# Attention and mixer kernel on one core: four small transfers moved to ScalarE's queue, and the last two batches and the late weight decoding in another order

## The chip, the cores and the metric

The kernel runs on one core of a Trainium2 chip. The metric is device time in microseconds (us). TensorE is written PE, VectorE DVE, ScalarE ACT, GpSimd POOL and SyncE SP. PEld is TensorE's loading of stationary operands, which overlaps PE.

## The reference

Eight batches of eight heads of causal attention with a decay, over 576 positions of 64 channels, and behind it a token mixer and a channel mixer:

```python
scores = q @ k.T / sqrt(64) + cum[:, None] - cum[None, :]   # cum = cumsum(log(clip(f)))
attn   = softmax(where(causal, scores, -1e9))
x      = concat_heads(attn @ v)                             # 8 x 576 x 512
h      = relu(x.T @ w_tok1) @ w_tok2                        # 576 -> 256 -> 576, over positions
u      = x + h.T
out    = u + relu(u @ w_ch1) @ w_ch2                        # 512 -> 1536 -> 512
```

Everything is float32. The four weights reach the kernel as 64-bit floats, in pairs of 32-bit words, and are decoded on the chip.

## The kernel before, in words

**Two-part products.** Most matrix products split a float32 operand into a high part and a rest (the tiles ending in h and l, or `p`, `hid`, `ring`, which hold both). ACT copies the high part (L351), and DVE (L360, or L363 with a ReLU) or POOL (L357) subtracts it from the operand. Three matmuls then stand for one.

**One head.** Q and K of a pair of heads arrive as `raw`, are split into `hl` (L546 and L556 or L548 and L556), and are gathered by SP transfers (L600) into the operands `k1` and `k2`. Rows of the decay come from `cc`, the running sum of log f, by small transfers (L594). PE makes the scores (L627), DVE masks them and takes row minima (L634), ACT takes exponentials (L641), DVE makes reciprocals (L659, L662) and POOL scales the rows (L669). PE transposes them (L683), ACT and DVE split them (L351, L360), and PE multiplies by V (L753 to L765). The products go into `xt` (L803 to L813). The first two heads are different (`FQ=2`): Q and K go into `xt`'s second tile as plain float32 (L604), and their two decay rows each are four transfers of one row (L589).

**The mixer of one batch.** In two halves: transposes (L984), first token product (`tok1`, L1017 to L1020) with its ReLU (L363), second (`tok2`, L1041 to L1043), the sum with x (L1055), then on the first 256 hidden channels `ch1` (L1086 to L1088) with its ReLU, and `ch2` (L1114 to L1116). The sums go to DRAM (`ud`, `pd`).

**The last part.** The other 1280 hidden channels are done after all attention, in nine chunks of 512 columns. A chunk has ten steps. The step's "up" is twelve matmuls with `w1r` (L900 to L902), then a ReLU split into `hid` (ACT L351, DVE L363), and its "down" is twelve with `w2r` (L921 to L923).

**Late decoding.** `w1r` and `w2r`, ten of each, are decoded into space that attention has used, so it can't begin before the last heads have let go of their buffers. Each of the 20 pieces is loaded as `d_raw` (L429), taken by ACT (L441), worked on by DVE in five instructions of 512 columns (L445, L449, L453, L457, L461), copied by ACT (L351) and completed by DVE (L360): six DVE instructions a piece. The first of a kernel's weights (`w_tok`) go the same way early, in smaller pieces, with POOL doing two of the steps.

**What sets the order.** The kernel's Python code lists operations with a priority, a duration, the tiles that they need, and what they wait for. `Plan.run` (L188) then plays them on five engines: a free engine takes the ready operation with the lowest priority number. The order that results is what is built, and each engine works through its list in that order. The priorities come from tables of numbers: `STEP` by head, `EARLY` and `LATE` added for the first and the last batch, `MIX` with `MIXE` and `MIXL` for the mixer, and `DEC3` as the spacing of the late pieces (L837). Durations in the plan only shape the order.

**SP's transfers.** SP issues transfers in order. Each transfer belongs to one of eight counters (`DMAHW0` to `DMAHW7`), and is issued only when the earlier transfer on the same counter has landed.

Of the kernel before, what the change touches and what calls it, by code (L numbers as in the profile page):

```python
# [20 lines left out]
    n_ring=12, n_part=4, n_xt=2, n_d_raw=3, n_d_g=2, n_hid=3, DEC3=10.1, SPREAD=9.86, SPREADA=5.54,  # L21
# [4 lines left out]
    fpe=3.69, lo0=-44.75, fev=-192.41, u=-110.56, dec=70.59, dec2=33.11, dec3=34.58, cd=-12.6, vload=-16.33,  # L26
# [113 lines left out]
class Op:  # L140
    __slots__ = ("eng", "dur", "head", "tail", "lat", "fn", "prio", "bufs", "need", "outs", "ready", "start", "idx")


class Plan:
# [43 lines left out]
    def run(self, slots):  # L188
# [9 lines left out]
        n = 0  # L198
# [8 lines left out]
        tail = dma_at = 0.0  # L207
# [30 lines left out]
        while left:  # L238
            moved = False
            for e, lst in ready.items():  # L240
# [23 lines left out]
                engine_at[e] = end  # L264
                heapq.heappush(events, (end, heap_id, None))
# [44 lines left out]
def build(nc, env, dims):  # L310
# [60 lines left out]

    def decay():
# [50 lines left out]
    def decode(prio, loads, w, hi, lo, tok, late=None):  # L423
# [15 lines left out]
        def s1():  # L439
            low, high, g, e = tl()  # L440
            nc.scalar.activation(asf(g), asf(high), AF.Copy, scale=2.0**-112)  # L441
# [23 lines left out]
        p.op("DVE", d_dve(w, True) * (1.2 if late else 1.8), prio, s3, rd=[gb], wr=[(gb, 1)], bufs=[gb])  # L465
        p.op("DVE", d_dve(w) * (1.1 if late else 1.3), prio, s4, rd=rd, wr=[(gb, 1)], bufs=[rb, gb])
        p.op("DVE" if late else "POOL", d_dve(w) if late else d_ptt(w), prio, s5, rd=[(gb, 1)], wr=[gb], bufs=[gb])
        p.op("DVE", d_dve(w), prio, s6, rd=rd, wr=[gb], bufs=[rb, gb])
        p.op("ACT", d_act(w, False), prio, lambda: hi_act(hi(), asf(tl()[2])), rd=[gb, *([late] if late else [])], wr=[(tok, "h")], bufs=[gb])
        p.op(  # L470
# [366 lines left out]
    for i, fn in enumerate(third):  # L837
        fn(HB + 2 + PRM["DEC3"] * i + (OFF["dec3"] if i < 2 * PAIRS0 else 0.0))
# [464 lines left out]
```

## Time and profile before

| | |
|---|---|
| three runs | 1123.4, 1130.65, 1132.02 us; median 1130.65 |
| profiled execution | 1124.72 us; its span is 1122.6 us, so 2.1 us lie around it |
| busy | PE 1080.8, DVE 633.9, ACT 557.3, POOL 536.5 us |
| attention with its mixers | to about 625 us of the span |
| nine chunks of the last part | from there to the end |

The granted clock (PEclk) is TensorE's clock as a share of full speed. In this trace it is 1.00 or 0.50, with values between where a window holds both. A row of the timeline gives the start, the duration, the engine and line, what was done, and in brackets how long the engine had been idle and what ended that. Timelines merge neighbouring instructions of one line, with their count behind an x. A row of the windows view gives for a stretch its length, the busy time of each engine with instruction counts, the granted clock, the DMA engines' busy share, and GB/s.

### The profile page before, as it was taken

To read this page: it belongs to the slowest core of one execution; us is meant where nothing else is said; L and a number is where in the kernel's file an instruction comes from. 1 tells how busy PE (TensorE), PEld (TensorE's weight loads), DVE (VectorE), ACT (ScalarE), POOL (GpSimd) and SP (SyncE) were. 2 spreads that over 40 slices of the span, in tenths; PEclk is the share of its full clock that TensorE was granted. 3 is DMA by queue.
4 is the path that set the end of the run, shared out by engine and by line. 5 is a ranking of instruction groups with operands and counts; after the bars stand their busy time and mean duration, and the time that the engine had idled before them with its cause. 6 is when DMAs were issued, how large, how long until landed. Compare 5 with 4: busy or idle time off the path is not lost.

```text
span 1122.6 us, 18731 instructions
## 1 busy us (share of the span) xinstructions
PE 1080.8 (96%) x6442; PEld 943.4 (84%) x6442; DVE 633.9 (56%) x1618; ACT 557.3 (50%) x1441; POOL 536.5 (48%) x615
## 2 busy tenths in 40 slices
PE   7898989999999999999998899999999999999998
PEld 5567878999999999998998788888888888888886
DVE  5778989787878877887799971121212121111111
ACT  3776868788888878887884531111111111111110
POOL 4577897869778678786843103230303121111010
PEclk8898999999999999999998999999999999999999
DMA  8687877777787787786724514230303030302011
GB/s 212 148 206 147 206 192 206 210 187 193 194 203 203 178 210 190 193 220 151 183 105 139 184 61 142 69 114 1 113 1 112 1 112 1 113 11 65 21 55 38
DMA packets 70831, 148.43 MB, mean 132 GB/s; under 512 B 10008, under 2 KB 27416, under 8 KB 69712
## 3 DMA queue, kind: packets, MB, share of 16 engines
q1 hardware_dynamic: 70736, 147.23, 48.7%
q8 instruction: 51, 0.84, 0.3%
q14 instruction: 44, 0.36, 0.1%
HBM read 63.46 MB, written 28.31 MB: 82 GB/s over the span
## 4 chain that ended last, share of the span: by engine, by line
PE 76%; DMA 8%; DVE 6%; POOL 3%; SPq 3%; ACT 2%; issue 2%; DVEq 0%; ACTq 0%; POOLq 0%
PE bank L901 7%; PE bank L900 7%; PE bank L902 7%; PE pair L922 7%; PE pair L921 7%; PE pair L923 7%; DMA k<-hl 6%; PE bank L683 6%; PE bank L627 5%; PE pair L627 2%; PE pair L765 2%; PE pair L763 2%; POOL pr L669 2%; SPq L600 1%; PE bank L1017 1%
## 5 line engine op out<-in xcount | busy, mean ns | idle before, releaser
L363 DVE SCALAR_TENSOR_TENSOR hid<-bank,hid 128x512 fp32r<-128x512 f32 x90 | 62.2, 691 | 340.5 <-ACT hid L351 340.4
L357 POOL TENSOR_TENSOR ring<-xt,ring 128x512 fp32r<-128x512 f32 (+1 forms) x68 | 91.9, 1365 | 316.7 <-ACT ring L351 315.9
L351 ACT ACTIVATE hid<-bank 128x512 fp32r<-128x512 f32 x90 | 53.9, 599 | 342.7 <-PE bank L902 342.7
L669 POOL TENSOR_SCALAR pr<-pr,rec 128x576 f32<-128x576 f32 (+4 forms) x320 | 171.8, 556 | 42.6 <-DVE rec L662 33.2
L351 ACT ACTIVATE p<-bank 128x384 fp32r<-128x384 f32 (+2 forms) x300 | 128.4, 475 | 48.0 <-PE bank L683 46.3
L683 PE MATMUL bank<-ident,pr 128*128 128x128 f32 (+1 forms) x960 | 140.3, 280 | 2.2 <-POOL pr L669 1.4
L900 PE MATMUL bank<-ring,w1r 128*128 128x512 f32 x360 | 140.1, 389 | 0.0
L901 PE MATMUL bank<-ring,w1r 128*128 128x512 f32 x360 | 140.1, 389 | 0.0
L902 PE MATMUL bank<-ring,w1r 128*128 128x512 f32 x360 | 140.1, 389 | 0.0
L921 PE MATMUL pair<-hid,w2r 128*128 128x512 f32 x360 | 140.1, 389 | 0.0
L922 PE MATMUL pair<-hid,w2r 128*128 128x512 f32 x360 | 140.0, 389 | 0.0
L923 PE MATMUL pair<-hid,w2r 128*128 128x512 f32 x360 | 140.0, 389 | 0.0
L641 ACT ACTIVATE pr<-bank,nmin 128x320 f32<-128x320 f32 (+3 forms) x256 | 118.1, 469 | 24.0 <-DVE nmin L634 22.1
L683 PEld LDWEIGHTS bank<-ident,pr 128*128 128x128 f32 (+1 forms) x960 | 109.5, 133 | 14.0 <-issue 3.4
L360 DVE TENSOR_TENSOR p<-bank,p 128x384 fp32r<-128x384 f32 (+1 forms) x180 | 106.0, 593 | 26.7 <-ACT p L351 25.6
L634 DVE CUSTOM_DVE_ANT_0 bank<-bank,mask 64x64 f32<-64x64 f32 (+3 forms) x256 | 106.7, 433 | 21.5 <-PE bank L627 19.2
L627 PE MATMUL bank<-k 128*128 128x320 f32 (+1 forms) x496 | 91.2, 305 | 10.9 <-DMA k<-hl 5.9
L627 PEld LDWEIGHTS bank<-k 128*128 128x128 f32 x496 | 76.9, 182 | 25.0 <-DMA k<-hl 5.3
L876 POOL TENSOR_TENSOR part<-part,xt 128x512 f32<-128x512 f32 x36 | 46.5, 1300 | 77.3 <-DMA part<-pd 71.7
L921 PEld LDWEIGHTS pair<-hid,w2r 128*128 128x128 f32 x360 | 67.6, 188 | 14.1
L923 PEld LDWEIGHTS pair<-hid,w2r 128*128 128x128 f32 x360 | 67.6, 188 | 14.1
L901 PEld LDWEIGHTS bank<-ring,w1r 128*128 128x128 f32 x360 | 67.6, 188 | 13.9
(125 smaller groups left out, 2482.7 us busy)
## 6 DMA issues: line engine op xcount, KB each, us to landing
k<-hl SPq DMA_DIRECT2D x186, 288.0 KB
raw<-in_qk SPq DMA_DIRECT2D x31, 576.0 KB
vr<-in_v SPq DMA_DIRECT2D x32, 320.0 KB
ud<-xt SPq DMA_DIRECT2D x8, 1152.0 KB
pd<-part SPq DMA_DIRECT2D x32, 288.0 KB
out_t<-part SPq DMA_DIRECT2D x36, 256.0 KB
d_raw<-in_w_ch SPq DMA_DIRECT2D x12, 512.0 KB
d_raw<-in_w_ch SPq DMA_DIRECT2D x40, 128.0 KB
```

Of the source, the lines that this page charges most:

```text
L351: nc.scalar.activation(out, in_, func, scale=scale)
L627: nc.tensor.matmul(ps[:m, of : of + w], k[:, 0, i0 : i0 + m], k[:, 1, j0 : j0 + w], start=(x == 0), stop=(fq or x == 1))
L634: nc.vector.tensor_tensor_reduce(x, x, E["mask"][:m, a : a + w], -1.0 / D**0.5, 3e38, op0=ALU.add, op1=ALU.min, accum_out=E["nmin"][sm][:m ...
L641: nc.scalar.activation(at(pr)[:m, poff[t] : poff[t] + w], at(buf)[:m, of : of + w], AF.Exp, bias=E["nmin"][sm][:m, t : t + 1], scale=-1.0, ...
L669: nc.gpsimd.tensor_scalar(x, x, r, 0.0, op0=ALU.mult, op1=ALU.add)
L683: nc.tensor.transpose(out, at(pr)[:, poff[i] + start[j] : poff[i] + end[j]], E["ident"])
L900: nc.tensor.matmul(q, wh[:, c, :], h_, start=(c == 0), stop=False)
L901: nc.tensor.matmul(q, wl[:, c, :], h_, start=False, stop=False)
L902: nc.tensor.matmul(q, wh[:, c, :], l_, start=False, stop=(c == NC - 1))
L921: nc.tensor.matmul(q, wh, h_, start=(i == i0), stop=False)
L922: nc.tensor.matmul(q, wl, h_, start=False, stop=False)
L923: nc.tensor.matmul(q, wh, l_, start=False, stop=(i == NF - 1))
```

## The change

Four edits.

1. The four transfers of the float32 heads' decay rows leave SP's queue. ACT issues them, right ahead of its first instruction of the first decoded piece (`t1`, position 0). The plan still counts them on SP.
2. The tables. `EARLY`, `LATE`, `MIXE` and `MIXL` become `HEAD` and `MIXB`, with one row for each batch. The row of batch 0 holds `EARLY`'s numbers, those of batches 1 to 5 hold zeros as before, and those of batches 6 and 7 are new. `DEC3` goes from 10.1 to 26.65 and `OFF["dec3"]` from 34.58 to 78.27, which spreads the late pieces over larger priority numbers.
3. From batch 6 on (`PORT = 6`) the plan doesn't start an operation of POOL, or a DVE operation marked `port` (the decoding's DVE steps, and the subtraction in L556 where DVE does it), before the end that the plan has set for the last such operation. This is a rule of the plan alone. No wait is added in the program that runs.
4. In the late decoding the plan's factors of 1.2 and 1.1 on three DVE durations become 1.0.

```diff
-    n_ring=12, n_part=4, n_xt=2, n_d_raw=3, n_d_g=2, n_hid=3, DEC3=10.1, SPREAD=9.86, SPREADA=5.54,
+    n_ring=12, n_part=4, n_xt=2, n_d_raw=3, n_d_g=2, n_hid=3, DEC3=26.65, SPREAD=9.86, SPREADA=5.54,
...
-    fpe=3.69, lo0=-44.75, fev=-192.41, u=-110.56, dec=70.59, dec2=33.11, dec3=34.58, cd=-12.6, vload=-16.33,
+    fpe=3.69, lo0=-44.75, fev=-192.41, u=-110.56, dec=70.59, dec2=33.11, dec3=78.27, cd=-12.6, vload=-16.33,
...
-EARLY = dict(
...
-LATE = dict(
...
+HEAD = dict(
+    cd=(
+        (42.22, -3.16, 15.37, -9.18, 55.25, -12.47, -73.68, 11.62),
+        (0.0, 0.0, 0.0, 0.0, 0.0, 0.0, 0.0, 0.0),
...
+        (-18.17, 6.86, 10.93, -1.41, -16.23, 1.17, 0.15, -28.59),
+        (-0.06, -1.59, -4.28, -6.54, -12.25, 0.0, 32.34, 3.06),
+    ),
...
+PORT = 6
...
+        o.port = (port or eng == "POOL") and self.batch >= PORT
...
-                    if o.ready > t or (best is not None and (o.prio, o.idx) >= (best.prio, best.idx)):
+                    if o.ready > t or (o.port and port_at > t) or (best is not None and (o.prio, o.idx) >= (best.prio, best.idx)):
...
+                if o.port:
+                    port_at = end
...
         def s1():
             low, high, g, e = tl()
+
+            for k, n, x in fqr if tok == ("t1", first_tok) else ():
+                nc.scalar.dma_start(at(k)[D + x : D + x + 1, x, :], asf(at(cc)[n : n + 1, 2, :]))
             nc.scalar.activation(asf(g), asf(high), AF.Copy, scale=2.0**-112)
...
+        m2, m1 = (1.2, 1.1) if p.batch < PORT else (1.0, 1.0)
...
-        p.op("DVE", d_dve(w, True) * (1.2 if late else 1.8), prio, s2, wr=[gb], bufs=[gb])
+        p.op("DVE", d_dve(w, True) * (m2 if late else 1.8), prio, s2, wr=[gb], bufs=[gb], port=True)
...
-        o = {k: OFF[k] + x[h] + (EARLY[k][h] if b == 0 else 0.0) + (LATE[k][h] if b == B - 1 else 0.0) for k, x in STEP.items()}
+        p.batch = b
+        o = {k: OFF[k] + x[h] + HEAD[k][b % 8][h] for k, x in STEP.items()}
...
             if fq:
+
+                fqr.append((k2, n, x))
                 dma(
-                    n + o["cd"], lambda k2=k2, n=n, x=x: nc.sync.dma_start(at(k2)[D + x : D + x + 1, x, :], asf(at(cc)[n : n + 1, 2, :])),
+                    n + o["cd"], lambda: None,
                     2304, dur=650, rd=["c", "rows"], wr=[(k2, "d", x)], bufs=[k2, cc],
                 )
...
     for i, fn in enumerate(third):
+        p.batch = B if i >= 3 else 0
         fn(HB + 2 + PRM["DEC3"] * i + (OFF["dec3"] if i < 2 * PAIRS0 else 0.0))
```

The lists of the two programs, engine by engine, are the same up to batch 6, but for the four transfers. The rows below have the line number of their own program: L589 is L670 in the changed one, L568 is L800, L594 is L828, L600 is L834, L441 is L671, L546 is L777, L351 is L575, L360 is L584, L363 is L587, L1055 is L1290, and L445, L449, L453, L457 and L461 are L675, L679, L683, L687 and L691.

**SP at the start**, before. `xt_130` holds the float32 heads, `cc_178` the decay sums; `hl` to `k` are the gathers of the third and fourth heads.

```order
L594 DMA k_164<-cc_178 2x1x576 [waits DMAHW5_49]
L589 DMA xt_130<-cc_178 1x16x36 [waits DMAHW6_49]
L589 DMA xt_130<-cc_178 1x16x36 [waits DMAHW7_49]
L568 DMA raw_158<-in_qk 128x1152 [waits DMAHW0_49,DVE_49]
L600 DMA k_162<-hl_161 64x1152 [waits DMAHW1_49]
L600 DMA k_164<-hl_161 64x2x576 [waits DMAHW2_49]
L589 DMA xt_130<-cc_178 1x16x36 [waits DMAHW3_49]
L589 DMA xt_130<-cc_178 1x16x36 [waits DMAHW4_49]
L600 DMA k_162<-hl_161 64x2x576 [waits DMAHW5_49]
L600 DMA k_163<-hl_161 64x2x576 [waits DMAHW6_49]
```

In the changed program the four L589 rows are gone from SP, and ACT has them between the split of the first `hl` and the first decoding:

```order
L777 ACTIVATE hl_161<-raw_158 128x2x576 [waits DMAHW1_49]
L670 DMA xt_130<-cc_178 1x16x36 [waits DMAHW0_49,DVE_49,Pool_49]
L670 DMA xt_130<-cc_178 1x16x36 [waits DMAHW2_49,Pool_49]
L670 DMA xt_130<-cc_178 1x16x36 [waits DMAHW4_49]
L670 DMA xt_130<-cc_178 1x16x36 [waits DMAHW6_49]
L671 ACTIVATE d_g_146<-d_raw_143 128x256 [waits DMAHW5_49]
L671 ACTIVATE d_g_147<-d_raw_144 128x256
```

The two rows of the second float32 head (the last two on each list) move ahead of two gathers. On ACT they stand behind counters 4 and 6, whose earlier transfers are the first and the third of the four loads of `d_raw`.

**DVE at the end of `tok1` of batch 7**, before. The ReLU of `tok1` is `ring_137<-bank_65,ring_136`; `tok2` on PE waits for it.

```order
L360 TENSOR_TENSOR ring_141<-bank_68,ring_141 64x256
L1055 TENSOR_TENSOR xt_130<-bank_67,xt_130 128x288
L453 SCALAR_TENSOR_TENSOR d_g_146<-d_raw_144,d_g_146 128x512
L445 TENSOR_SCALAR d_g_147<-d_g_147 128x512
L457 TENSOR_TENSOR d_g_146<-d_g_146 128x512
L449 TENSOR_SCALAR d_g_147<-d_g_147 128x512
L461 SCALAR_TENSOR_TENSOR d_g_146<-d_raw_144,d_g_146 128x512
L453 SCALAR_TENSOR_TENSOR d_g_147<-d_raw_143,d_g_147 128x512
L363 SCALAR_TENSOR_TENSOR ring_137<-bank_65,ring_136 128x512
```

And in the changed program:

```order
L584 TENSOR_TENSOR ring_141<-bank_68,ring_141 64x256
L1290 TENSOR_TENSOR xt_130<-bank_66,xt_130 128x288
L1290 TENSOR_TENSOR xt_130<-bank_67,xt_130 128x288
L584 TENSOR_TENSOR w1r_6911<-d_g_146,w1r_6911 128x512
L675 TENSOR_SCALAR d_g_147<-d_g_147 128x512
L587 SCALAR_TENSOR_TENSOR ring_137<-bank_65,ring_136 128x512
```

Six instructions of the late decoding stood between the last sum and the ReLU, and now two.

**DVE between `ch1` and `ch2` of batch 7**, before. The first two L363 rows are the ReLU results that `ch2` on PE waits for.

```order
L449 TENSOR_SCALAR d_g_146<-d_g_146 128x512
L453 SCALAR_TENSOR_TENSOR d_g_146<-d_raw_145,d_g_146 128x512
L445 TENSOR_SCALAR d_g_147<-d_g_147 128x512
L457 TENSOR_TENSOR d_g_146<-d_g_146 128x512
L449 TENSOR_SCALAR d_g_147<-d_g_147 128x512
L461 SCALAR_TENSOR_TENSOR d_g_146<-d_raw_145,d_g_146 128x512
L453 SCALAR_TENSOR_TENSOR d_g_147<-d_raw_144,d_g_147 128x512
L457 TENSOR_TENSOR d_g_147<-d_g_147 128x512
L360 TENSOR_TENSOR w2r_7145<-d_g_146,w2r_7145 128x512
L363 SCALAR_TENSOR_TENSOR ring_137<-bank_67,ring_136 128x288
L363 SCALAR_TENSOR_TENSOR ring_142<-bank_66,ring_141 128x288
```

And in the changed program:

```order
L1290 TENSOR_TENSOR xt_130<-bank_65,xt_130 128x288
L691 SCALAR_TENSOR_TENSOR d_g_146<-d_raw_143,d_g_146 128x512
L687 TENSOR_TENSOR d_g_147<-d_g_147 128x512
L587 SCALAR_TENSOR_TENSOR ring_137<-bank_67,ring_136 128x288
L587 SCALAR_TENSOR_TENSOR ring_142<-bank_66,ring_141 128x288
L587 SCALAR_TENSOR_TENSOR ring_137<-bank_65,ring_136 128x288
```

Nine decoding instructions stood between the last sum and the ReLU, and now two. The work put off comes later: of the 120 DVE instructions of the late decoding, 64 stood ahead of the first `hid` row (L363, the ReLU split of the first up step), and now 48. Between the first `hid` row and the end of the last `w1r` piece there were 59 DVE rows in all (both ends counted), and now 77. PE's list around this place keeps its shape: 28 matmuls of `tok1`, 24 of `tok2`, 48 of `ch1`, 30 of `ch2`, then up, up, down, up, down and so on.

More of the change, by code (lines that the diff above doesn't have):

```diff
@@ L107 @@
+HEAD = dict(
+    cd=(
[8 rows of a table added]
+    ),
+    kh=(
[8 rows of a table added]
+    ),
+    kl=(
[8 rows of a table added]
+    ),
+    s4=(
[8 rows of a table added]
+    ),
+    s3=(
[8 rows of a table added]
+    ),
+    s2=(
[8 rows of a table added]
+    ),
+    mn=(
[8 rows of a table added]
+    ),
+    ex=(
[8 rows of a table added]
+    ),
+    rec=(
[8 rows of a table added]
+    ),
+    nrm=(
[8 rows of a table added]
+    ),
+    t3=(
[8 rows of a table added]
+    ),
+    t2=(
[8 rows of a table added]
+    ),
+    t1=(
[8 rows of a table added]
+    ),
+    t0=(
[8 rows of a table added]
+    ),
+    hl=(
[8 rows of a table added]
+    ),
+    av=(
[8 rows of a table added]
+    ),
+    fold=(
[8 rows of a table added]
+    ),
+    load=(
[8 rows of a table added]
+    ),
+    vload=(
[8 rows of a table added]
+    ),
+    qh=(
[8 rows of a table added]
+    ),
+    ql=(
[8 rows of a table added]
+    ),
+    vh=(
[8 rows of a table added]
+    ),
+    vl=(
[8 rows of a table added]
+    ),
+    lo0=(
[8 rows of a table added]
+    ),
 )
@@ L140 @@
 class Op:
-    __slots__ = ("eng", "dur", "head", "tail", "lat", "fn", "prio", "bufs", "need", "outs", "ready", "start", "idx")
+    __slots__ = ("eng", "dur", "head", "tail", "lat", "fn", "prio", "bufs", "need", "outs", "ready", "start", "idx", "port")
 class Plan:
@@ L461, in s6 @@
             nc.vector.scalar_tensor_tensor(g, high, 0x80000000, g, op0=ALU.bitwise_and, op1=ALU.bitwise_or)
+        m2, m1 = (1.2, 1.1) if p.batch < PORT else (1.0, 1.0)
         p.op("ACT", d_act(w, False), prio, s1, rd=rd, wr=[gb], bufs=[rb, gb])
[L464 to L468 removed]
+        p.op("DVE", d_dve(w, True) * (m2 if late else 1.8), prio, s2, wr=[gb], bufs=[gb], port=True)
+        p.op("DVE", d_dve(w, True) * (m2 if late else 1.8), prio, s3, rd=[gb], wr=[(gb, 1)], bufs=[gb], port=True)
+        p.op("DVE", d_dve(w) * (m1 if late else 1.3), prio, s4, port=True, rd=rd, wr=[(gb, 1)], bufs=[rb, gb])
+        p.op("DVE" if late else "POOL", d_dve(w) if late else d_ptt(w), prio, s5, port=True, rd=[(gb, 1)], wr=[gb], bufs=[gb])
+        p.op("DVE", d_dve(w), prio, s6, port=True, rd=rd, wr=[gb], bufs=[rb, gb])
         p.op("ACT", d_act(w, False), prio, lambda: hi_act(hi(), asf(tl()[2])), rd=[gb, *([late] if late else [])], wr=[(tok, "h")], bufs=[gb])
@@ L572, in build @@
                 el, d_lo(el, 2 * S), n + o["ql"], lambda hl=hl, raw=raw, el=el: lo_on(el, at(hl)[:, 1::2, :], at(raw), at(hl)[:, 0::2, :]),
-                rd=[raw, (hl, 0)], wr=[(hl, 1)], bufs=[hl, raw],
+                rd=[raw, (hl, 0)], wr=[(hl, 1)], bufs=[hl, raw], port=True,
             )
@@ L1135, in mixer @@
     for i, (c, f) in enumerate(us):
-        f(n + 1 + PRM["LAG"] + o["fpe"] + MIX[part][i] + (MIXE[part][i] if b == 0 else 0.0) + (MIXL[part][i] if b == B - 1 else 0.0) + (PRM["SPREAD"] if part else PRM["SPREADA"]) * done / total)
+        f(n + 1 + PRM["LAG"] + o["fpe"] + MIX[part][i] + MIXB[b % 8][part][i] + (PRM["SPREAD"] if part else PRM["SPREADA"]) * done / total)
         done += c
```

98 lines of the change are left out of this document (39 added, 59 removed), and 188 rows, old and new, of tables (av, cd, ex, fold).

## The prediction

> **What bounds the kernel now.** I read the page first, then the windows, then the timelines of single engines where PE stops.
>
> ```profile
> span 1122.6 us, 18731 instructions
> ...
> PEclk8898999999999999999998999999999999999999
> ```
>
> ```profile
> 0.00:28.00 28.00, 22.27 (x175) 16.12 (x175) 15.71 (x46) 11.01 (x26) 13.37 (x26) 0.84 0.86 212
> 252.00:280.00 28.00, 28.00 (x219) 26.92 (x218) 21.88 (x67) 24.00 (x67) 25.51 (x32) 1.00 0.73 188
> 588.00:616.00 28.00, 24.58 (x171) 24.18 (x170) 25.77 (x40) 12.87 (x23) 8.72 (x6) 0.88 0.42 146
> 616.00:644.00 28.00, 23.99 (x114) 20.57 (x113) 27.66 (x48) 14.53 (x28) 4.47 (x4) 0.94 0.54 171
> 644.00:672.00 28.00, 28.00 (x125) 23.21 (x124) 22.37 (x40) 9.89 (x16) 0.00 (x0) 1.00 0.23 75
> ```
>
> In the middle and in the last part PE is busy all the time at full clock: the end moves with PE's lost time and with nothing else. PE loses time at the start and in the handover to the last part, both by pauses and by a halved clock. In the handover DVE is almost full, so PE's pauses there are DVE's. Each us that PE gains at one of these places reaches the end, if nothing behind it makes PE wait again.
>
> **The start: the decay rows.**
>
> ```profile
> 14.91 2.71 SPq L589 DMA_DIRECT2D xt<-cc  x2
> 17.67 1.34 SPq L600 DMA_DIRECT2D k<-hl  x2
> ```
>
> ```profile
> 15.73 6.11 DMA xt<-cc
> ```
>
> ```profile
> 15.86 2.23 PE L627 MATMUL bank<-xt 66*128 66x448 f32 x8
> 21.97 3.95 PE L627 MATMUL bank<-xt 66*128 66x320 f32 x8 [3.88 <-DMA xt<-cc]
> 25.85 2.24 PE L627 MATMUL bank<-k 128*128 128x320 f32 x8
> ```
>
> The second head's rows are issued at 14.91 and 15.73, and the last lands 6.11 us later; PE has nothing from 18.09 (15.86 and 2.23) to 21.97. The change issues them on ACT. How early, and what do they push?
>
> ```profile
> 7.11 1.15 ACT L546 ACTIVATE hl<-raw 128x1152 fp32r<-128x1152 f32 x1
> 10.28 0.81 ACT L441 ACTIVATE d_g<-d_raw 128x256 f32<-128x256 f32 x2 [2.03 <-DMA d_raw<-in_w_tok]
> 18.76 0.30 ACT L641 ACTIVATE pr<-bank,nmin 64x64 f32<-64x64 f32 x1
> ```
>
> ```profile
> 15.77 0.59 DVE L445 TENSOR_SCALAR d_g<-d_g 128x256 uint32<-128x256 uint32 x1 [0.81 <-ACT d_g L441]
> 16.29 0.75 DVE L634 CUSTOM_DVE_ANT_0 pair<-pair,mask 128x576 f32<-128x576 f32 x1
> ```
>
> ACT is free at 8.26 and idles for 2.03 us until `d_raw` has landed. The first two transfers fit there. The other two wait on counters whose earlier transfers are loads of `d_raw`, so they go out at about 10 to 10.7. ACT's price for one isn't in the trace; the nearest rows are SP's, 0.67 for a gather (1.34 for two). ACT starts decoding at about 11.3, 1.0 us later (bounds 0 and 1.4). The first head's rows aren't missed, since PE works through its warm-up matmuls until then. Those of the second, even at 6.11 us from an issue at 11.3, land at 17.4, ahead of 18.09.
>
> What is late next? The decode chain is pushed by 1.0 us, and L445 at 15.77 stands ahead of the first head's minima (16.29) on DVE. The exponentials follow by the same 1.0, and PE's next eight matmuls write the bank that the exponential at 18.76 frees, at 19.06. So PE resumes near 20.2 and not at 21.97: **1.75 us**. The third head's gathers are no new wait. The first SP row behind the moved ones, 17.67, goes out nearly 4 us earlier, and PE wants its data only after eight matmuls.
>
> The clock is the other half.
>
> ```profile
> 20.00:24.00 4.00, 2.03 (x5) 1.67 (x6) 0.58 (x3) 0.68 (x3) 3.04 (x6) 0.50 1.04 239
> ...
> 32.00:36.00 4.00, 4.00 (x24) 3.21 (x25) 3.62 (x13) 3.18 (x10) 1.82 (x3) 0.90 0.02 6
> ```
>
> The mean of 0.90 puts the return to full speed at 32.8. From 21.97 that is 10.8 us at half speed, a loss of 5.4 us. The same kind of eight matmuls took 2.23 us ahead of the pause and 3.95 behind it. Does a shorter pause keep the clock?
>
> ```profile
> 39.80:43.20 3.40, 2.38 (x18) 1.80 (x17) 2.49 (x6) 3.06 (x10) 2.93 (x6) 1.00 1.01 243
> 43.20:46.60 3.40, 3.40 (x19) 1.96 (x18) 1.79 (x5) 0.89 (x3) 3.31 (x7) 1.00 0.98 210
> 524.30:527.70 3.40, 1.65 (x11) 1.21 (x9) 3.00 (x9) 2.30 (x9) 0.91 (x1) 1.00 0.59 146
> 527.70:531.10 3.40, 3.37 (x12) 3.11 (x13) 1.16 (x5) 1.23 (x4) 3.24 (x2) 0.50 0.47 134
> ```
>
> The clock changes on a grid of about 3.4 us. A stretch with 1.02 us of idle (3.40 less 2.38) left it alone; one with 1.75 (524.3 to 527.7) halved it for the next. The remaining pause of 2.1 us (18.09 to 20.2) halves it if most of it falls into one stretch, which I take as likelier than not, with one stretch of half speed less than now: 3.4 us at half speed, 1.7 us saved. Value for the start 1.75 + 1.7 = **3.5**; bounds 1.75 (same slow stretch) and 7.2 (none). I let it pass whole to where PE is full, since what follows hangs on PE and on transfers that start behind PE's work.
>
> The Trainium skill ("TensorE: Matmul & The Clock Gate", Part 1) has a free-running window of about 3.4 us and a fall to half rate after an idle window. The grid agrees; the rows above fall after half a window of idle, so the measurement decides. By the page no pause that is left would halve the clock, and that outcome is the second rival.
>
> **The handover to the last part.**
>
> ```profile
> 603.95 0.61 PE L1041 MATMUL bank<-t2h,ring 128*128 128x288 f32 x1 [3.42 <-DVE ring L363]
> ...
> 620.33 0.61 PE L1114 MATMUL bank<-ring,w2h 128*128 128x288 f32 x1 [4.01 <-DVE ring L363]
> ```
>
> ```profile
> 600.57 0.60 ACT L351 ACTIVATE ring<-bank 128x512 fp32r<-128x512 f32 x1 [1.45 <-PE bank L1018]
> 617.64 0.63 ACT L351 ACTIVATE w2r<-d_g 128x512 fp32r<-128x512 f32 x1 [3.81 <-DVE d_g L461]
> ```
>
> ```profile
> 598.32 1.27 DVE L453 SCALAR_TENSOR_TENSOR d_g<-d_raw,d_g 128x512 f32<-128x512 uint32 x1
> 603.22 0.68 DVE L363 SCALAR_TENSOR_TENSOR ring<-bank,ring 128x512 fp32r<-128x512 f32 x1
> 614.90 1.77 DVE L457 TENSOR_TENSOR d_g<-d_g 128x512 f32<-128x512 f32 x1
> ```
>
> ACT had the first ReLU done at 601.17, and DVE came to its own at 603.22, after the six decoding instructions of the list. With two ahead, which are ready earlier, the pause is ACT's 0.60 and DVE's 0.68 with hand-offs, about 1.6: **1.8 saved** of 3.42. At the second, ACT itself stood behind a decoding copy that waited 3.81 us for DVE; with two instructions in place of nine, I keep 1.0 for ReLU and hand-offs: **3.0 saved** of 4.01.
>
> The clock there: PE works at half speed from 603.95 to about 609.7 (the mean of 0.77 below puts the return there) and from 620.33 to 623.3.
>
> ```profile
> 606.00:614.00 8.00, 8.00 (x49) 8.00 (x49) 6.08 (x9) 3.53 (x6) 3.61 (x3) 0.77 0.56 210
> ...
> 619.90:623.30 3.40, 2.97 (x12) 2.97 (x13) 3.37 (x7) 2.39 (x6) 1.40 (x2) 0.50 0.78 211
> ```
>
> That costs half of 5.7 and of 2.97, so 2.9 and 1.5. A pause of 1.0 spares the second; 1.6 stands at the edge of what halved it above, so half of the first: **2.9 saved**.
>
> Put-off decoding takes some back.
>
> ```profile
> L360 DVE TENSOR_TENSOR w1r<-d_g,w1r x10: 673/681/691, 573.0 to 662.7; 128x512 fp32r<-128x512 f32 x10
> ```
>
> ```profile
> 629.75 0.68 DVE L363 SCALAR_TENSOR_TENSOR hid<-bank,hid 128x512 fp32r<-128x512 f32 x1
> ```
>
> ```profile
> 625.74 0.42 PE L900 MATMUL bank<-ring,w1r 128*128 128x512 f32 x1
> ...
> 672.04 0.39 PE L900 MATMUL bank<-ring,w1r 128*128 128x512 f32 x1
> ```
>
> The last `w1r` is ready at 663.4 and PE wants it at 672.04: 8.6 us of slack. From the first `hid` row to there DVE worked off 59 rows in 33.6 us, 0.57 each. Now there are 77, 43.9 us. Counted from PE's first up (625.74, with `hid` 4.0 later) the piece is ready after 47.9 us and wanted after 46.3: **1.6 lost**. Bounds: nothing, and 6.2 at the rate of the stretch ahead (573.0 to 629.75, 90 rows, 0.63 each). The handover is worth 1.8 + 3.0 + 2.9 - 1.6 = **6.1** (bounds 0 and 9).
>
> **Batches 6 and 7.** Other rows there I price at 0: the same work in another order, and PE full but for the pause at 526. That one cost 1.75 and half of a 3.4 us stretch, 3.4 in all; it may vanish or get a twin, so bounds of -3.4 and +3.4. Edit 4 acts only through the order.
>
> **Sum.** 3.5 + 6.1 = 9.6 us off the profiled execution's 1124.7 gives 1115.1. The three runs have their median at 1130.65, and all four together a mean of 1127.7: runs differ by 8 us, about what one slow stretch at the start and one later cost, so I take it for the clock's grid falling differently. 1127.7 - 9.6 = **1118**.
>
> **The rivals.**
>
> *The clock falls as before.* Both places lose their pauses but not their slow stretches: 1.75 and 1.8 + 3.0 - 1.6 = 5 in all, 1123. For: 2.1 us is more than what halved it elsewhere.
>
> *The clock never falls.* Start 7.2, handover 1.8 + 3.0 + 4.4 - 1.6 = 7.6: 1113. For: the grid is free, and a pause can straddle it.
>
> *The hold-apart does not hold.* It binds the plan only.
>
> ```profile
> 613.40 2.72 POOL L357 TENSOR_TENSOR ring<-xt,ring 128x512 fp32r<-128x512 f32 x2 [0.46 <-ACT ring L351]
> ```
>
> While POOL ran this, DVE's L457 took 1.77 (the mean of all 18 is 0.746, below). If POOL's work meets the decoding as before, the handover gives most back at 0.63 a row: 6.1 - 4.6 = 1.5, and 1123. The Trainium skill ("SBUF — State Buffer", Who interferes with whom) calls the port that these two share an exclusive lock that goes to whoever starts first. The row agrees, and no list order forbids the meeting.
>
> *Slower.* The decoding falls behind PE.
>
> ```profile
> L453 DVE SCALAR_TENSOR_TENSOR d_g<-d_raw,d_g 128x512 f32<-128x512 uint32 x18 | 15.5, 863 | 0.2
> L457 DVE TENSOR_TENSOR d_g<-d_g 128x512 f32<-128x512 f32 x18 | 13.4, 746 | 0.2
> ```
>
> Place: DVE from the first `hid` on. At 0.80 a row, the mean of these two, 77 rows take 61.6 and PE waits 19.3 us over the chunk's steps. It decides once a row costs over 0.70 (then 11.6 are lost, and start and handover's 7.7 + 3.5 = 11.2 are gone); the price would be 8 us net, 1136, and 1139 with a twin of the pause at 526. Against: behind 626 POOL has next to nothing to do (0.00 from 644).
>
> **How the numbers follow.** Forecast 0.45, clock as before 0.17, clock never 0.12, hold-apart fails 0.18, slower 0.08. About 1% is what a measurement can tell here, so faster means below 1119.3. The forecast lies near that line, and I give it three fifths of its chance there (0.28), the clock-never case all (0.12), the two at 1123 a quarter (0.09): faster 0.49. Slower by 1% needs 1142, so the price above on one of the slower runs: 0.04 of its case and 0.01 from elsewhere, 0.05. The rest, 0.46, is within 1%. The range, from the clock-never case with a twin gone and a fast run to the hold-apart case on a slow run, is 1106 to 1131.
>
> **What would show it.** Right: ACT issues four transfers near 8 to 11 us; PE's wait at 22 us for `xt<-cc` is gone and its next one is shorter than 2.5 us; the pauses ahead of L1041 and L1114 (L1276 and L1349 in the changed program) are below 2 us and wait for L363's ReLU only; the last `w1r` ends less than 3 us after PE wants it. Wrong: a wait for the exponentials as long as the old one, half clock to 33 us, PE waiting for `w1r` or `w2r` over 5 us in the first chunk, or a new wait for gathers in batches 6 and 7.

## The result, and the profile after

The changed kernel takes 1118.94 us (median of 6 runs, 1116.05 to 1120.4). The kernel before took 1130.57 us (median of 6). The ratio is 0.9898, with a 95% interval of 0.9875 to 0.9920: about 11.5 us faster. 1118.0 was predicted, with a range of 1106 to 1131. The total came out right, but for reasons that only partly hold. One execution among those reported below, the profiled one of the kernel `POOL waits`, took 2114.74 us and is left out of all medians and ratios.

The page of the changed kernel first: its span and the granted clock in 40 slices.

```profile
span 1116.7 us, 18738 instructions
...
PEclk8898999999999999999999999999999999999999
```

Behind the fourth slice (112 us) no slice has a clock below 9, where before there was one of 8 near 600 us. The spans differ by 5.9 us (1122.6 less 1116.7), half of the difference of the medians. To find where, I took from PE's timelines when the same piece of work starts: the first matmul of `tok1` in a batch, and the first up step of the last part (us).

| | batch 0 | batch 1 | batch 6 | batch 7 | first up |
|---|---|---|---|---|---|
| before | 78.02 | 157.53 | 508.35 | 583.64 | 625.74 |
| after | 78.69 | 163.68 | 515.55 | 587.94 | 619.96 |
| after less before | +0.7 | +6.2 | +7.2 | +4.3 | -5.8 |

The changed kernel is 7.2 us behind when batch 6 comes, though up to there its lists differ in four transfers only. Then it gains 2.9 in batch 6 and 10.1 from batch 7 to the last part. So three places have to be explained.

**The start.** The timeline of ACT in the changed kernel (ACTq is its sequencer, which issues the transfers), and PE's:

```profile
8.57 1.17 ACT L777 ACTIVATE hl<-raw 128x1152 fp32r<-128x1152 f32 x1 [2.36 <-DMA raw<-in_qk]
8.66 4.21 ACTq L670 DMA_DIRECT2D xt<-cc  x4
12.92 0.76 ACT L671 ACTIVATE d_g<-d_raw 128x256 f32<-128x256 f32 x2 [3.18 <-DMA xt<-cc]
```

```profile
21.75 3.98 PE L861 MATMUL bank<-xt 66*128 66x320 f32 x8 [3.21 <-ACT pr L875]
```

The wait for the rows is gone, and a wait for the exponentials stands in its place: PE resumes 0.2 us earlier. In this execution `raw` landed late (ACT waited 2.36 us for it, where before it had not waited), which pushed the whole chain.

**Between 84 and 112 us.** The windows view, then the timelines of DVE, POOL and PE in the changed kernel:

```profile
84.00:112.00 28.00, 18.06 (x110) 16.06 (x109) 24.37 (x52) 15.23 (x42) 19.44 (x23) 0.82 0.63 147
```

```profile
104.30 6.52 DVE L679 TENSOR_SCALAR d_g<-d_g 128x256 uint32<-128x256 uint32 x1
```

```profile
101.25 5.58 POOL L903 TENSOR_SCALAR pr<-pr,rec 128x576 f32<-128x576 f32 x10
106.80 2.74 POOL L581 TENSOR_TENSOR ring<-xt,ring 128x576 fp32r<-128x576 f32 x2
109.52 1.14 POOL L779 TENSOR_SCALAR hl<-raw 128x1152 fp32r<-128x1152 f32 x1
```

```profile
111.61 1.11 PE L917 MATMUL bank<-ident,pr 128*128 128x128 f32 x4 [5.56 <-DVE p L584]
```

DVE's decoding step of 256 columns took 6.52 us and ended at 110.82, just behind POOL's run of 13 instructions without a gap, which ended at 110.66. The same step takes 0.28 us elsewhere (94.42, for one). PE stood for 5.56 us. A smaller meeting of the same kind lies ahead of it: L691 at 89.91 took 2.34 us, where its twins take 0.42, and PE waited 2.39 us at 93.40. In the profile before, the instruction of 104 us met only the end of POOL's run:

```profile
102.75 2.60 DVE L449 TENSOR_SCALAR d_g<-d_g 128x256 uint32<-128x256 uint32 x1
```

```profile
102.43 2.77 POOL L357 TENSOR_TENSOR ring<-xt,ring 128x576 fp32r<-128x576 f32 x2
```

**The handover.** The windows of the changed kernel, and the rows of PE and DVE that answer to those of the prediction:

```profile
588.00:616.00 28.00, 26.05 (x198) 25.25 (x198) 24.34 (x44) 14.68 (x28) 9.87 (x7) 1.00 0.40 136
616.00:644.00 28.00, 28.00 (x137) 23.83 (x136) 26.02 (x46) 14.28 (x26) 4.00 (x4) 1.00 0.57 174
644.00:672.00 28.00, 28.00 (x126) 23.22 (x125) 25.79 (x48) 12.52 (x21) 1.28 (x1) 1.00 0.29 94
```

```profile
606.21 0.40 PE L1276 MATMUL bank<-t2h,ring 128*128 128x288 f32 x1 [1.41 <-DVE ring L587]
...
619.96 0.40 PE L1135 MATMUL bank<-ring,w1r 128*128 128x512 f32 x1
...
668.28 0.39 PE L1135 MATMUL bank<-ring,w1r 128*128 128x512 f32 x1
```

```profile
605.46 0.69 DVE L587 SCALAR_TENSOR_TENSOR ring<-bank,ring 128x512 fp32r<-128x512 f32 x1 [2.29 <-ACT ring L575]
...
666.71 0.69 DVE L584 TENSOR_TENSOR w1r<-d_g,w1r 128x512 fp32r<-128x512 f32 x1
```

DVE now waits for ACT's ReLU, instead of the ReLU waiting for DVE. The pause ahead of `tok2` is 1.41 us, the one ahead of `ch2` is gone, the clock is 1.00 all through, and PE is full from 616 on.

### The profile page after: what moved, and what is told of

Read it like the earlier page. It is cut to its first block, busy times and chain, and to the rows that moved or that the text cites. A ratio compares the mean times of both kernels' runs of the same rounds, so it can differ in the third digit from the quotient of the medians.

```text
span 1116.7 us, 18738 instructions
## 1 busy us (share of the span) xinstructions
PE 1076.1 (96%) x6442; PEld 939.2 (84%) x6442; DVE 633.4 (57%) x1618; ACT 557.8 (50%) x1441; POOL 536.7 (48%) x615
## 4 chain that ended last, share of the span: by engine, by line
PE 77%; DVE 7%; DMA 7%; POOL 3%; ACT 2%; SPq 2%; issue 1%; DVEq 0%; POOLq 0%; ACTq 0%
PE bank L1135 7%; PE bank L1136 7%; PE bank L1137 7%; PE pair L1156 7%; PE pair L1158 7%; PE pair L1157 7%; PE bank L917 6%; DMA k<-hl 6%; PE bank L861 5%; PE pair L861 2%; PE pair L997 2%; PE pair L999 2%; PE bank L1276 1%; PE bank L1278 1%; PE pair L987 1%
## 5 line engine op out<-in xcount | busy, mean ns | idle before, releaser
L587 DVE SCALAR_TENSOR_TENSOR hid<-bank,hid 128x512 fp32r<-128x512 f32 x90 | 62.2, 691 | 337.1 <-ACT hid L575 336.9
L575 ACT ACTIVATE hid<-bank 128x512 fp32r<-128x512 f32 x90 | 53.8, 598 | 344.2 <-PE bank L1137 344.2
L575 ACT ACTIVATE p<-bank 128x384 fp32r<-128x384 f32 (+2 forms) x300 | 128.5, 476 | 41.3 <-PE bank L917 38.9
L875 ACT ACTIVATE pr<-bank,nmin 128x448 f32<-128x448 f32 (+3 forms) x256 | 118.3, 469 | 26.0 <-DVE nmin L868 23.8
L584 DVE TENSOR_TENSOR p<-bank,p 128x384 fp32r<-128x384 f32 (+1 forms) x180 | 106.1, 594 | 27.5 <-ACT p L575 26.4
L1137 PEld LDWEIGHTS bank<-ring,w1r 128*128 128x128 f32 x360 | 67.6, 188 | 14.1
L1136 PEld LDWEIGHTS bank<-ring,w1r 128*128 128x128 f32 x360 | 67.6, 188 | 14.0
```

The lines of the kernel that those rows point to most:

```text
L575: nc.scalar.activation(out, in_, func, scale=scale)
L875: nc.scalar.activation(at(pr)[:m, poff[t] : poff[t] + w], at(buf)[:m, of : of + w], AF.Exp, bias=E["nmin"][sm][:m, t : t + 1], scale=-1.0, ...
L1136: nc.tensor.matmul(q, wl[:, c, :], h_, start=False, stop=False)
L1137: nc.tensor.matmul(q, wh[:, c, :], l_, start=False, stop=(c == NC - 1))
```

## The experiments

The theory from the two traces: the gain is the hold-apart's, at the handover; edit 1 brings next to nothing; the stall at 104 us hides half of the gain in this pair of profiles. The rivals: edit 1 brings 3.5 us (the prediction's); the new tables as such bring the gain; the stall is chance.

| kernel | median us (runs) | ratio to before | 95% interval |
|---|---|---|---|
| changed, again | 1116.36 (4) | 0.9883 | 0.9846 to 0.9921 |
| rows back on SP | 1118.39 (6) | 0.9895 | 0.9865 to 0.9926 |
| before with rows on ACT | 1127.87 (12) | 0.9981 | 0.9961 to 1.0001 |
| no hold-apart | 1128.23 (12) | 0.9983 | 0.9962 to 1.0005 |
| old tables | 1119.94 (6) | 0.9910 | 0.9892 to 0.9928 |
| old spacing | 1120.24 (5) | 0.9924 | 0.9896 to 0.9951 |
| hold-apart alone | 1121.14 (6) | 0.9933 | 0.9908 to 0.9958 |
| hold-apart from batch 0 | 1198.85 (4) | 1.0612 | 1.0571 to 1.0653 |
| 32 fills | 1116.26 (4) | 0.9894 | 0.9859 to 0.9930 |
| POOL waits | 1113.19 (5) | 0.9878 | 0.9841 to 0.9914 |
| POOL waits, 16 fills | 1115.48 (8) | 0.9902 | 0.9867 to 0.9937 |
| both steps through, 16 fills | 1114.56 (6) | 0.9881 | 0.9858 to 0.9903 |

**Edit 1 undone.**

```diff
-            for k, n, x in fqr if tok == ("t1", first_tok) else ():
+            for k, n, x in ():
...
-                    n + o["cd"], lambda: None,
+                    n + o["cd"], lambda k2=k2, n=n, x=x: nc.sync.dma_start(at(k2)[D + x : D + x + 1, x, :], asf(at(cc)[n : n + 1, 2, :])),
```

> The changed kernel with the four decay rows back on SP (edit 1 undone); the lists of PE, DVE and POOL are those of the changed kernel. By the prediction's start step (edit 1 is worth 3.5 us): 1118.9 + 3.5 = about 1122.5 us, with a wait of some 3.9 us for xt<-cc near 22 us. By the theory from the two traces (edit 1 is worth about 0.2 us at 33 us, and it shifts DVE by 1 to 2.6 us against POOL, so that an instruction of 0.28 us took 6.52 us at 104 us and PE stood 5.6 us): 1112 to 1115 us, and no PE wait above 3 us between 84 and 112 us. By a third theory (that meeting of DVE and POOL is chance in each execution, whoever issues the rows): 1118 to 1120 us, with the long instruction in some executions of this kernel too.

1118.39 us: the third theory's number. With the rows on SP the stall is there as well, on DVE's timeline and POOL's:

```profile
104.45 6.52 DVE L679 TENSOR_SCALAR d_g<-d_g 128x256 uint32<-128x256 uint32 x1
```

```profile
109.68 1.14 POOL L779 TENSOR_SCALAR hl<-raw 128x1152 fp32r<-128x1152 f32 x1
```

So edit 1 doesn't cause it, and my theory fell in that point.

**Edit 1 alone.** The kernel before, with the rows issued ahead of L441.

```diff
-    cc = Buf("cc")
+    cc = Buf("cc"); fqr = []; first_tok = 0
...
-            nc.scalar.activation(asf(g), asf(high), AF.Copy, scale=2.0**-112)
+            [nc.scalar.dma_start(at(k)[D + x : D + x + 1, x, :], asf(at(cc)[n : n + 1, 2, :])) for k, n, x in (fqr if tok == ("t1", first_tok) else ())]; nc.scalar.activation(asf(g), asf(high), AF.Copy, scale=2.0**-112)
...
-                dma(
-                    n + o["cd"], lambda k2=k2, n=n, x=x: nc.sync.dma_start(at(k2)[D + x : D + x + 1, x, :], asf(at(cc)[n : n + 1, 2, :])),
+                fqr.append((k2, n, x)); dma(
+                    n + o["cd"], lambda: None,
```

> The kernel before with edit 1 alone (four decay rows issued on ACT). By the prediction's start step: 1130.6 - 3.5 = about 1127 us. By the theory from the traces: nothing gained at 33 us (within 0.5 us), and the DVE instruction near 104 us that waits out POOL's work is there as in the changed kernel, so 1130 to 1136 us. If the meeting is chance, 1130 us, within 1.

1127.87 us: 2 us less than before, and the interval just holds no change. Over the nine profiles with the same early lists and no fills, the start reads: PE resumes at 21.97, 22.34 and 23.05 with the rows on SP (before, edit 1 undone, hold-apart alone), and at 20.05, 20.36, 20.40, 20.86, 21.07 and 21.75 with the rows on ACT. The means are 22.45 and 20.75: the pause gives 1.7, and not the 0.2 that I read in one profile. The clock stood at 0.50 for four stretches of 3.4 us in three of the six, as with the rows on SP, and for three stretches in the other three.

**No hold-apart.**

```diff
-        o.port = (port or eng == "POOL") and self.batch >= PORT
+        o.port = False
```

> The changed kernel without edit 3: the plan holds nothing apart, the tables, the spacing and the factors stay. The late decoding's DVE rows move forward again (72 rows of 512 columns ahead of the first hid row, as before the change; 56 in the changed kernel). If the handover's gain comes from the decoding standing behind the ReLUs, the pauses ahead of the second token product and the second channel product come back, and with them most of the gain: 1127 to 1133 us. If it comes from the new tables of batches 6 and 7 as such: 1118 to 1121 us.

(The counts of decoding rows in these expectations include eight 512-column rows of the early decoding; without them they are 64 before and 48 in the changed kernel.) 1128.23 us: with the tables, the spacing and edit 1, but without edit 3, the gain is gone. PE's timeline has both pauses back:

```profile
604.85 0.61 PE L1276 MATMUL bank<-t2h,ring 128*128 128x288 f32 x1 [4.29 <-DVE ring L587]
...
620.31 0.61 PE L1349 MATMUL bank<-ring,w2h 128*128 128x288 f32 x1 [3.62 <-DVE ring L587]
```

**Old tables, old spacing, and hold-apart alone.** Rows of batches 6 and 7 as before; `DEC3` and `dec3` as before; both of these and the rows back on SP.

```diff
-PORT = 6
+PORT = 6; HEAD = {k: r[:6] + ((0.0,) * 8, LATE[k]) for k, r in HEAD.items()}
```

```diff
-    n_ring=12, n_part=4, n_xt=2, n_d_raw=3, n_d_g=2, n_hid=3, DEC3=26.65, SPREAD=9.86, SPREADA=5.54,
+    n_ring=12, n_part=4, n_xt=2, n_d_raw=3, n_d_g=2, n_hid=3, DEC3=10.1, SPREAD=9.86, SPREADA=5.54,
```

(With the old `LATE` ahead of the first; `MIXB` and `OFF["dec3"]` likewise.)

> The changed kernel with the rows of batches 6 and 7 in the tables as before (zeros for batch 6, the old late table for batch 7); spacing, hold-apart and edit 1 stay. 63 rows of late decoding stand ahead of the first hid row (before 72, changed 56). If holding apart and the spacing carry the gain: 1119 to 1122 us. If the new rows of the tables carry it: 1127 us or more, with pauses of 2 us or more between 500 and 625 us.

> The changed kernel with the spacing of the late decoding as before (DEC3 10.1, dec3 34.58); tables, hold-apart and edit 1 stay. 64 of the 512-column decoding rows stand ahead of the first hid row (before 72, changed 56). If holding apart is what carries the gain: 1119 to 1121.5 us. If the spacing is needed for it: 1124 us or more, with the pauses of 3 to 4 us ahead of the second token product or the second channel product back.

> The kernel before with the plan's hold-apart alone (edits 3 and 4): tables and spacing as before, rows on SP. 61 decoding rows stand ahead of the first hid row (before 72, changed 56). If holding apart carries the gain by itself: 1119 to 1123 us. If it needs the new tables or the spacing: 1125 us or more.

1119.94, 1120.24 and 1121.14 us. Hold-apart alone (with edit 4) is worth 7.6 us (0.67% of 1128, interval 4.7 to 10.4); everything but edit 3 is worth 1.9 (-0.6 to 4.3); all together 11.5. The two parts come to 9.5, and these intervals can't tell that from 11.5. From the first `tok1` of batch 7 to the first up it took 42.10, 40.73 and 43.47 us without hold-apart (before, edit 1 alone, no hold-apart), and 32.02, 31.98, 32.05, 33.58, 33.63 and 36.30 with it (changed, again, rows on SP, old tables, hold-apart alone, old spacing). That is where the gain is made, in all nine.

**The changed kernel again** (no edit), and **hold-apart from batch 0**.

```diff
-PORT = 6
+PORT = 0
```

> The changed kernel itself again, as the control for the comparisons on this chip: 1116 to 1121 us. If the long DVE instruction near 104 us (6.52 us for work of 0.28 us) belongs to the program, its profile has it again and PE waits 5 to 6 us there; if it is chance, it is gone and the profile is about 5 us shorter. At the start, ACT's first decoding at 11.2 to 12.1 us and PE's third group of scores near 20.0 to 20.9 us, as in the three kernels above with the rows on ACT; 12.9 and 21.75, as in the first profile, if that was no accident of the raw load.

> The changed kernel with PORT = 0: the plan holds POOL and the decoding's DVE steps apart in all batches, so for the early decoding as well. If the plan's times are near enough to the chip's there, the DVE instruction that waits out POOL near 104 us and PE's wait of 5.6 us behind it are gone: 1112 to 1115 us. Rival: the tables of batches 0 to 5 were made for another order, and the early decoding is held up by POOL's longer runs; PE waits elsewhere between 60 and 200 us by as much or more: 1119 to 1135 us.

The first has the stall again (6.51 us at 104.50); ACT decodes from 12.24 and PE resumes at 21.07. In the second no decoding step takes more than 1.66 us (at 687; six others took 1.23 to 1.63), as meant, and it is 80 us slower than the changed kernel: batch 1's `tok1` begins at 229.22 in place of 163.68. The table of the early batches belongs to another order; the rule without a matching table costs far more than the meetings do.

**Fills.** Small matmuls ahead of the second float32 head's scores.

```diff
-            ps = at(buf)
-            m, i0 = size[t], start[t]
+            ps = at(buf); E["n_sc"] = E.get("n_sc", 0) + 1
+            m, i0 = size[t], start[t]; [nc.tensor.matmul(E["av"][("b2", "b3")][:64, :48], E["ident"][:, :64], E["ident"][:, :48], start=True, stop=True) for _ in range(32 if E["n_sc"] == 6 else 0)]
```

> The changed kernel with 32 small matmuls (of the kind of the warm-up, into a bank that is not in use yet) ahead of the second float32 head's scores, so that PE has about 2.1 us of work in the pause near 18 to 20 us. If that pause is what halves the clock to 32 us, the clock stays at 1.00 there, the eight matmuls take 2.2 us and not 3.97, and PE's work at 22 to 32 us, 10 us at half speed, is up to 5 us earlier, unless the masks and exponentials set the pace: 1114 to 1118 us. If the clock falls by what lies ahead (PE's idle time before 18 us) or the masks and exponentials set the pace: 1118 to 1121 us.

The windows with fills, and in the changed kernel's second profile:

```profile
20.00:24.00 4.00, 4.00 (x52) 3.56 (x50) 1.40 (x7) 1.74 (x9) 2.66 (x5) 1.00 1.06 215
24.00:32.00 8.00, 6.84 (x44) 5.31 (x43) 7.65 (x30) 6.42 (x21) 2.38 (x5) 1.00 0.66 148
```

```profile
20.00:24.00 4.00, 2.93 (x6) 1.81 (x6) 2.59 (x11) 2.35 (x9) 2.04 (x3) 0.53 1.05 205
24.00:32.00 8.00, 8.00 (x28) 5.71 (x28) 5.23 (x20) 4.78 (x17) 1.92 (x6) 0.50 0.74 167
```

A filled pause keeps the clock at 1.00: the pause is what halves it. At the first `tok1` the kernel is 3.2 us ahead (75.27 against 78.44), though the 32 fills ran for 3.93 us and made PE 1.5 us late (scores at 22.61, against 21.07). At the end the times don't differ (1116.26 and 1116.36).

**A real wait for POOL** on one step of the piece (`w1`, 2), alone and with 16 fills in place of 32. The step's line is L678 here, and L679 is POOL's.

```diff
-            low, high, g, e = tl()
-            nc.vector.tensor_scalar(e, g, 0xFF800000, None, op0=ALU.bitwise_and)
+            low, high, g, e = tl(); nc.vector.tensor_scalar(e, g, 0xFF800000, None, op0=ALU.bitwise_and)
+            nc.gpsimd.tensor_scalar(E["warm"], asf(e)[:, :1], 1.0, None, op0=ALU.mult) if tok == ("w1", 2) else None
```

> The changed kernel with one more POOL instruction (128x1, into a tile that nothing reads) behind the first row scaling of the second head near 104 us; it reads what the long DVE instruction writes, so POOL waits there until DVE is through. If that instruction takes 6.5 us because POOL's run of instructions has no gap, it now ends within 1.5 us, PE's wait of 5.6 us behind it shrinks to under 1.5 us, and the time is 1113 to 1115 us. If PE's wait there has another cause (POOL's row scaling itself is late), or POOL's lost time comes back as a wait for POOL: 1117 to 1120 us.

> The kernel above with 16 small matmuls ahead of the second float32 head's scores (32 in the kernel with fills took 3.93 us and kept the clock at 1.00 from 16 to 44 us, but PE came 1.7 us late to the scores). If the two effects add: 3 to 5 us less than the kernel above, 1109 to 1112 us, with the clock at 1.00 from 16 to 40 us and no halved stretch near 101 to 108 us. If the fill is too short to keep the clock or the gain is lost before 100 us: within 1 us of the kernel above.

1113.19 us (five runs, 1110.62 to 1120.69) and 1115.48 us. The effects don't add at the end: with the fills 1109 to 1112 was expected. The only trace of the first is of the execution of 2114.74 us, with PE busy for 2101.5 us of it, and says nothing of this place. Timelines of DVE and POOL with the 16 fills:

```profile
98.07 0.67 DVE L678 TENSOR_SCALAR d_g<-d_g 128x256 uint32<-128x256 uint32 x1
...
100.68 4.30 DVE L683 SCALAR_TENSOR_TENSOR d_g<-d_raw,d_g 128x256 f32<-128x256 uint32 x1
```

```profile
98.82 0.22 POOL L679 TENSOR_SCALAR warm<-d_g 128x1 f32<-128x1 f32 x1 [0.24 <-DVE d_g L678]
...
103.56 1.14 POOL L779 TENSOR_SCALAR hl<-raw 128x1152 fp32r<-128x1152 f32 x1
```

A gap of 0.24 us on POOL let the first step through. The next one met the rest of POOL's run and took 4.30 us, to the end of it; PE waited 4.13 us. So I put that one right behind the first, ahead of POOL's wait (16 fills again):

```diff
-            low, high, g, e = tl(); nc.vector.tensor_scalar(e, g, 0xFF800000, None, op0=ALU.bitwise_and)
+            low, high, g, e = tl(); nc.vector.tensor_scalar(e, g, 0xFF800000, None, op0=ALU.bitwise_and); tok == ("w1", 2) and s4(1)
...
-        def s4():
+        def s4(early=0):
...
-            nc.vector.scalar_tensor_tensor(asf(e), low, 2.0**-52, asf(e), op0=ALU.mult, op1=ALU.mult)
+            (early or tok != ("w1", 2)) and nc.vector.scalar_tensor_tensor(asf(e), low, 2.0**-52, asf(e), op0=ALU.mult, op1=ALU.mult)
```

> The kernel with the 16 fills and POOL's wait, with the next DVE instruction of that piece put right behind the one that POOL waits for: both are through before POOL goes on. In the kernel with the wait alone the one took 0.67 us and the next 4.30, ending with POOL's run, and PE waited 4.1 us. If POOL's run without a gap is the cause, no DVE instruction between 96 and 112 us takes over 1.6 us, PE has no wait over 2 us there, and PE's first exponentials of the seventh head are 2 to 4 us earlier than in that kernel. The time: 1111 to 1114 us if this reaches the end; 1114 to 1117 us if it is lost again between 500 and 545 us, where that kernel gave its lead back (a wait of 2.1 us for gathers, 35.99 us for a stretch that took 32.6 to 33.8 in six other profiles).

```profile
98.54 0.86 DVE L678 TENSOR_SCALAR d_g<-d_g 128x256 uint32<-128x256 uint32 x1
99.43 0.43 DVE L683 SCALAR_TENSOR_TENSOR d_g<-d_raw,d_g 128x256 f32<-128x256 uint32 x1
```

The stall is gone; the smaller meeting ahead of it is still there (2.61 us at 83.90). That kernel reaches the first `tok1` of batch 1 at 155.99, against 163.68, and that of batch 4 at 368.34 against 380.58: 12.2 us ahead. At the first up 5.6 are left (614.38). Of the 6.6 lost, 4.7 are PE's waits for gathers (5.7 us between the two landmarks, against 1.0), and 1.7 are one stretch at half clock from 505.8, which the changed kernel hasn't got. Between 300 and 545 us the waits of that kernel and of the changed one (total, times, longest) are:

```profile
PE bank L861 <- DMA k<-hl: 6.1, 6, 2.0
```

```profile
PE bank L861 <- DMA k<-hl: 1.6, 4, 0.5
```

Its median, 1114.56 us, is 4.4 and 1.8 below the changed kernel's two, but the intervals of their ratios overlap, and so does that of the kernel with POOL's wait alone (1113.19); that any of them beats the changed kernel is not shown. What limits the gathers there is open.

## Why the prediction was right, and where it was not

**The total.** That it came out within 1 us is luck in part: the start was put 1.5 to 3.5 us too high, the handover 4.3 too low, and the base 2.9 below the later median. (Three fifths of 0.45 is 0.27 and not 0.28, so the chance of faster should have been 0.48.)

**The base.** The prediction started from a profile of 1124.7 us and put the 6 us to the median down to the clock's grid. That step failed. The stall at 104 us takes 4.86 to 6.71 us in the nine other profiles whose early lists are the same (but for the rows, the fills at the start, or both) and hold no wait for POOL, two of them with the rows on SP (without hold-apart it is the step ahead, L675, that is held); the profile of before had the 2.60 us quoted above. It was the exception. That row, nine times as long as its twins, was the warning, and I didn't read it. The mean of four runs was still a good base (1127.7, where the later medians of the kernel before are 1127.9 to 1130.6), but not for the reason given.

**The start, 3.5.** The pause's 1.75 holds: 1.7 over nine profiles, with the wait turned to the exponentials, as predicted. ACT's decoding began at 11.2 to 12.9 (predicted 11.3): four issues took 3.95 to 4.86 us, waits included, against the 2.03 us that ACT had idled for `d_raw`. The clock's 1.7 came in three profiles of six. Of all this the times show 2 us for edit 1 alone, and nothing where it is undone.

**The handover, 6.1.** Right in place and cause, too small by 4.3. Saved ahead of `tok2` 2.0 (predicted 1.8), ahead of `ch2` 4.0 (3.0): the wait is gone altogether, and with it my 1.0 for hand-offs; the first ReLU is through at 614.66, and PE comes to `ch2` at 615.89. Clock 4.4 (2.9): the pause of 1.41 halved nothing here. Put-off decoding 0 (1.6 lost). The last `w1r` was ready at 667.40, 47.4 us after the first up, where 47.9 was predicted at 0.57 a row. But PE wants it at 668.28, after 48.3 us and not after 46.3: its list now has 21 down matmuls between that up and the one ahead of it, where it had 12. The order part before the prediction said that the list keeps its shape; it does for the first steps only. The sum is 10.4, and the table of landmarks has 10.1.

**Batches 6 and 7, 0.** 2.9 gained in this pair of profiles, inside the bounds. The pause at 526 us is gone here, but the kernel before with edit 1 alone hasn't got it either, in the old order (its longest wait for gathers behind 500 us is 0.4); so it isn't the order's doing alone.

**The rival "the hold-apart does not hold".** It binds the plan only, and holds well enough. Of the 84 to 90 decoding steps of 512 columns behind 500 us that stand singly in the timeline, 9 to 11 are stretched by more than 0.1 us without it, by 8.8 to 9.0 us in all (three profiles); with it 6 or 7, by 3.7 to 6.0 (seven profiles). What it does besides is to take the decoding out from ahead of the ReLUs: without it, 64 rows stand ahead of the first `hid` again. No run parts these two effects, and either could carry much of the gain. In the profile before, two of the six steps ahead of the first ReLU took 1.8 us longer than their twins (598.32 and 599.51), and four of the nine ahead of the second 4.2 us (610.36 to 616.67); the pauses that went are 2.0 and 4.0. In the changed kernel both steps ahead of the second ReLU are still stretched, by 2.1 us in all, but PE has `ch1` to do until 615.89.

**Two rules.** By the Trainium skill's page "TensorE: Matmul & The Clock Gate" (Part 1), where the clock falls after an idle window of about 3.4 us, no pause that was left at the start or the handover would halve it. The runs disagree: a pause of 1.11 us (old tables) was followed by three stretches at half speed. What tells it from the 1.41 us ahead of `tok2`, behind which the clock stayed at 1.00, no run shows.

```profile
20.40 3.44 PE L861 MATMUL bank<-xt 66*128 66x320 f32 x8 [1.11 <-ACT pr L875]
```

The Trainium skill's page "SBUF — State Buffer" (Who interferes with whom) gives the shared port of DVE and POOL to whoever issues first, for the whole instruction. The runs agree that one waits for the other, and at 104 us they show a longer wait: DVE's step waited through the rest of POOL's run, from 104.30 to 110.82, over eight of POOL's instructions. It isn't so everywhere. In the changed kernel's handover two steps each got through behind a single POOL instruction (they ended at 611.35 and 613.20), though POOL's four show no gap between 609.89 and 616.15:

```profile
610.34 1.56 DVE L691 SCALAR_TENSOR_TENSOR d_g<-d_raw,d_g 128x512 uint32<-128x512 uint32 x1
611.82 1.93 DVE L687 TENSOR_TENSOR d_g<-d_g 128x512 f32<-128x512 f32 x1
```

What tells the two cases apart is open.

## What to carry to other kernels

Compare a profile's own time with the median before building on it; if they differ by more than the effect looked for, look for an instruction whose duration is several times that of its twins. Where two engines share a resource, read the end of the long instruction against the end of the other engine's run: when the two agree within 0.2 us, the one probably waited for the other. Here a gap of 0.24 us on the other engine let one step through and left the next to wait 4.30; an order that keeps the two apart paid in the last batches and cost 80 us where the tables didn't fit it. And a lead gained early need not reach the end: follow the same piece of work through both traces, landmark by landmark.

## What was not expected of the hardware

- At 104 us a DVE step of 0.28 us waited as long as POOL had instructions without a gap (6.5 us), and went through in the first gap (0.24 us). At 610 us steps got through behind single instructions of a run without a gap.
- A pause of PE of 1.1 to 4.6 us at the start halved the clock for 10.2 or 13.7 us in all nine profiles without fills that were read there, though PE was busy again; filled with small matmuls, the clock stayed.
- The same first load (`raw`, issued at 1.40 us) let ACT begin its split of it between 6.53 and 8.57 us.
